# A Mamba-2 scan followed by a gated MLP: seven-product matmuls in three more steps, state updates moved to GpSimd, and another order of loads and of the head

## The chip, the cores and the metric

The kernel runs on one NeuronCore of a Trainium2 chip. Its engines work side by side, each through its own instructions in order: TensorE (PE in the profile, its weight loads PEld), VectorE (DVE), ScalarE (ACT), GpSimd (POOL) and SyncE (SP), which issues DMA transfers; ACT's queue can issue them too. The metric is device time in microseconds (us) of one execution, the median of several runs. Less is better.

## What is computed

The reference has two parts. The first is a chunked state-space scan over 4 batches, 8 heads and 768 positions, with a state of 16 x 32 per head:

```python
L = np.exp(cum[:, :, :, None] - cum[:, :, None, :]) * causal
M = np.einsum('bhin,bhjn->bhij', Cc, Bc) * L
y_intra = np.einsum('bhij,bhjd->bhid', M, xc)
y_inter = np.einsum('bhin,bhnd->bhid', Cc, state) * decay_to_i[:, :, :, None]
y[:, :, sl] = y_intra + y_inter
state = decay_full[:, :, None, None] * state + np.sum(Bx, axis=2)
```

Its output, as 3072 tokens of 256 features, goes through the second part, with w_in of 256 x 2048 and w_out of 2048 x 256, all in fp32:

```python
h = x @ w_in
g = h * np.cos(h)
return (g @ w_out).astype(np.float32)
```

## The kernel before

The sequence is cut into six chunks of 128 positions (NC = 6), each of two halves of 64 (W = 64). For each chunk the MLP runs 16 steps (NF = 16), numbered n = 16 c + f with chunk c and step f in it. A step multiplies 256 columns of w_in with half of the chunk's tokens (512 columns of the result, hp, in PSUM), forms the gate, and multiplies it with w_out into o. While chunk c goes through the MLP, the scan of chunk c + 1 is worked in between.

The order of every engine is written out by hand, in the loop over n from line 1114. In a step PE does hp of step n (`first`, L672, or `first7`, L772) and then o of step n - 2 (`second`, L808, or `seven`, L848; LAG = 2). Between them lies a chain over three engines: `wind_k` (ACT, L679), `wind_w` (DVE, L685), `gate` (ACT's sine, L694), `gated` (DVE, L699, writes gT), and from chunk 1 on `differ` (POOL, L724 to L727), which forms the four combinations gd of gT.

A product of two 2 x 2 block matrices takes eight block products, or seven with sums and differences of the blocks beforehand and of the results afterwards. From chunk 1 on `seven` does so for o: the differences of w_out are made once (`differ_w`), those of the gate by `differ`, and the results are summed per unit of eight steps (`rest`, L873, on POOL one part per step; then stores, L876). For hp `first7` does the same in the steps that `runs` (L1034) lists: steps 9 to 13 of chunks 2 to 4, and steps 1 to 13 of chunk 5. It needs the differences of w_in (`differ_in`, L743) and of y (`differ_y`, L754), and it ends in four additions on DVE (L785, L788, L790, L793) and a copy on ACT (L779). In a run the gate of step n is formed while hp of step n + 1 is made (`late`), and both pairs of PSUM banks with the tag "scan" belong to the run.

The scan's parts for chunk c + 1 are placed by the table `steps` (L1006), by step f of chunk c: `reach` (cumulated decays, DVE, L586), `turn` (transposes of B and C, DVE, L594), then one step later `turn2` (copies of C on ACT, L603, and the product rT on DVE, L605), `inner` (PE, L615), `weigh` (DVE, L477), `state` (the states carried on, DVE, L510), `decays` (scans of 512 columns, DVE, L387, from rows that `load_arow` fetches), `along` (loads of a for `reach`). `open2` (PE, L629, reads the states and rT) stands in step 14, `finish2` (PE, L641) in step 15.

SP's queue is in order too: a store that waits for its sum (L876) holds up the loads issued after it. `block_loads` places the loads of B and C for the transposes, `load` those of x and B by half, `rest_of_loads` those of the weights' last pieces, the rows of a and the third and fourth half.

The head, lines 285 to 302 and 909 to 946, is the scan of chunk 0 in two units of 64 positions. Loads: C by ACT in four parts (`load_c`), a, B, x and weights by SP (`fetch`). C is copied (L358 on POOL, a quarter on ACT, L918), turned (L407) and scaled (`take_c`, L411). `spread_a` (PE, L376) and `decays0` (DVE, L387) make the decays, `inner` (L468) the products of B and C, `weights` (L477) multiplies them. `finish0` (L489 to L537) makes y and the state, and its copy to yT is what hp reads. Weights arrive as words and are prepared by `grade` (ACT, L258 and L256; POOL, L259) and `join` (DVE, L271, L275; POOL, L283).

## Time and profile before

| what | us |
|---|---|
| median of 3 runs | 364.64 |
| lowest and highest run | 363.92, 365.25 |
| the profiled execution, its own time | 364.44 |
| its span, first to last instruction | 362.7 |

In the profile PE is busy in nearly every slice of the span but the first microseconds; the granted clock is 0.998 of full speed. Where the busy time of the costliest groups lies:

| line, engine | what | count | busy us | mean ns |
|---|---|---|---|---|
| L672 PE | hp, ordinary, 128x256 | 544 | 129.6 | 382 |
| L848 PE | o by seven products, 128x128 (largest group) | 474 | 66.0 | 275 |
| L772 PE | hp by seven products, 128x128 (largest group) | 168 | 23.4 | 276 |
| L685, L699 DVE | w and gT, 128x512 | 96 each | 65.8, 65.6 | 686, 683 |
| L724, L726, L727 POOL | gd | 79 each | 58.1, 39.6, 39.0 | 735, 501, 493 |
| L586 DVE | reach scans, 128x64 | 32 | 10.3 | 368 |
| L510 DVE | states, 128x64 (largest group) | 24 | 8.7 | 419 |
| L605 DVE | rT, 128x256 | 8 | 4.1 | 507 |

Matmuls overlap, so the mean of one is longer than the distance between two starts; a matmul in fp32 appears as two instructions. A line of the timeline or of the chain gives start and duration in us from the span's start.

### The profile page before, as it was taken

To read this page: it belongs to the slowest core of one execution; us is meant where nothing else is said; L and a number is where in the kernel's file an instruction comes from. 1 tells how busy PE (TensorE), PEld (TensorE's weight loads), DVE (VectorE), ACT (ScalarE), POOL (GpSimd) and SP (SyncE) were. 2 spreads that over 40 slices of the span, in tenths; PEclk is the share of its full clock that TensorE was granted. 3 is DMA by queue.
4 is the path that set the end of the run, shared out by engine and by line. 5 is a ranking of instruction groups with operands and counts; after the bars stand their busy time and mean duration, and the time that the engine had idled before them with its cause. 6 is when DMAs were issued, how large, how long until landed. Compare 5 with 4: busy or idle time off the path is not lost.

```text
span 362.7 us, 10240 instructions
## 1 busy us (share of the span) xinstructions
PE 357.0 (98%) x4070; PEld 326.0 (90%) x4070; DVE 276.0 (76%) x504; ACT 184.0 (51%) x352; POOL 239.7 (66%) x387
## 2 busy tenths in 40 slices
PE   8999999999999999999999999999999999999995
PEld 4788888889999999999989999999999999999995
DVE  7779998488876987878766877875776776688864
ACT  3597656544454346534536533545553544444552
POOL 5567767699666677674786666686666465475572
PEclk9999999999999999999999999999999999999999
DMA  7984997666583429113228202110001001001001
GB/s 138 246 284 141 189 196 122 85 125 98 134 129 58 99 51 135 14 34 76 53 53 119 23 3 75 28 33 11 0 2 31 0 3 33 0 3 29 3 17 44
DMA packets 96624, 26.43 MB, mean 73 GB/s; under 512 B 86624, under 2 KB 92480, under 8 KB 96576
## 3 DMA queue, kind: packets, MB, share of 16 engines
q1 hardware_dynamic: 95328, 25.38, 34.9%
q8 instruction: 32, 0.52, 0.6%
q10 hardware_dynamic: 1248, 0.39, 0.5%
q14 instruction: 16, 0.13, 0.1%
HBM read 22.36 MB, written 3.34 MB: 71 GB/s over the span
## 4 chain that ended last, share of the span: by engine, by line
PE 96%; DMA 2%; DVE 1%; issue 0%; ACT 0%; POOL 0%; DVEq 0%
PE o L848 35%; PE hp L672 33%; PE o L808 8%; PE m L772 7%; PE hp L772 5%; DMA bc<-in_C_dram 2%; PE y L641 2%; PE g L615 1%; PE y L489 1%; PE y L629 1%; PE g L468 1%; PE y L537 1%; PE y L527 1%; PE o L900 0%; PE tp L451 0%
## 5 line engine op out<-in xcount | busy, mean ns | idle before, releaser
L672 PE MATMUL hp<-yT,w_in 128*128 128x256 f32 x544 | 129.6, 382 | 0.1
L672 PEld LDWEIGHTS hp<-yT,w_in 128*128 128x128 f32 x544 | 99.0, 190 | 13.8 <-issue 1.4
L724 POOL TENSOR_TENSOR gd<-gT 128x256 f32<-128x256 f32 x79 | 58.1, 735 | 76.9 <-DVE gT L699 61.8
L694 ACT ACTIVATE w<-w,quarter 128x512 f32<-128x512 f32 x96 | 69.4, 723 | 65.8 <-DVE w L685 65.7
L685 DVE SCALAR_TENSOR_TENSOR w<-hp,k 128x512 f32<-128x512 f32 x96 | 65.8, 686 | 45.4 <-ACT k L679 45.2
L679 ACT ACTIVATE k<-hp 128x512 int32<-128x512 f32 x96 | 57.2, 596 | 68.6 <-PE hp L672 60.3
L699 DVE TENSOR_TENSOR gT<-hp,w 128x512 f32<-128x512 f32 x96 | 65.6, 683 | 12.2 <-ACT w L694 8.3
L848 PE MATMUL o<-words,gd 128*128 128x128 f32 x474 | 66.0, 275 | 0.0
L848 PEld LDWEIGHTS o<-words,gd 128*128 128x128 f32 x474 | 59.4, 192 | 0.0
L848 PE MATMUL o<-w_out,gT 128*128 128x128 f32 x316 | 50.4, 278 | 0.0
L848 PEld LDWEIGHTS o<-w_out,gT 128*128 128x128 f32 x316 | 45.4, 191 | 3.1
L726 POOL TENSOR_TENSOR gd<-gT,gd 128x128 f32<-128x128 f32 x79 | 39.6, 501 | 6.2
L727 POOL TENSOR_TENSOR gd<-gT,gd 128x128 f32<-128x128 f32 x79 | 39.0, 493 | 6.2
L848 PE MATMUL o<-w_out,gd 128*128 128x128 f32 x158 | 30.6, 276 | 0.0
L848 PE MATMUL o<-words,gT 128*128 128x128 f32 x158 | 30.6, 275 | 0.0
L808 PE MATMUL o<-w_out,gT 128*128 128x256 f32 x128 | 30.0, 380 | 0.0
L387 DVE TENSOR_TENSOR_SCAN lam<-arow,unit 128x512 f32<-128x512 f32 x20 | 29.9, 1496 | 0.1
L808 PEld LDWEIGHTS o<-w_out,gT 128*128 128x128 f32 x128 | 24.2, 190 | 3.6 <-POOL w_out L283 0.4
L848 PEld LDWEIGHTS o<-words,gT 128*128 128x128 f32 x158 | 24.0, 192 | 0.0
L848 PEld LDWEIGHTS o<-w_out,gd 128*128 128x128 f32 x158 | 24.0, 192 | 0.0
L772 PE MATMUL m<-m,words 128*128 128x128 f32 x168 | 23.4, 276 | 0.0
L772 PE MATMUL hp<-yT,w_in 128*128 128x128 f32 x112 | 21.7, 275 | 0.0
(130 smaller groups left out, 463.6 us busy)
## 6 DMA issues: line engine op xcount, KB each, us to landing
words<-in_moe_w_in_dram SPq DMA_DIRECT2D x8, 512.0 KB
words<-in_moe_w_out_dram SPq DMA_DIRECT2D x8, 512.0 KB
xr<-in_x_dram SPq DMA_DIRECT2D x24, 128.0 KB
arow<-a_cut SPq DMA_DIRECT2D x10, 256.0 KB
arow<-a_cut SPq DMA_DIRECT2D x10, 252.0 KB
out_dram<-sum SPq DMA_DIRECT2D x18, 128.0 KB
bc<-in_B_dram SPq DMA_DIRECT2D x24, 64.0 KB
blocks<-in_B_dram SPq DMA_DIRECT2D x16, 32.0 KB
```

The lines of the kernel that those rows point to most:

```text
L387: V.tensor_tensor_scan(out=lams[k][:, p, hs].rearrange(flat), data0=rows_.rearrange(flat), data1=unit0[:, hs].rearrange(flat), initial=0.0 ...
L672: PE.matmul(to_[:, e], lhsT=w_in[:, k, fs], rhs=y[:, k], start=(k == 0), stop=(k == KT - 1), skip_group_check=True)
L679: ACT.activation(k, hp[n], AF.Copy, bias=0.25, scale=INV_2PI)
L685: V.scalar_tensor_tensor(out=w, in0=hp[n], scalar=INV_2PI, in1=k, op0=ALU.mult, op1=ALU.subtract)
L694: ACT.activation(cos, cos, AF.Sin, bias=quarter, scale=TWO_PI)
L699: V.tensor_tensor(out=gT[n], in0=hp.pop(n), in1=cos, op=ALU.mult)
L724: G.tensor_tensor(out=d[:, 0:2], in0=g[:, 1:2].to_broadcast([P, 2, P]), in1=g[:, 3::-3], op=ALU.subtract)
L726: G.tensor_tensor(out=d[:, 2], in0=g[:, 0], in1=d[:, 0], op=ALU.subtract)
L727: G.tensor_tensor(out=d[:, 3], in0=g[:, 2], in1=d[:, 2], op=ALU.subtract)
L772: PE.matmul(dst[q], lhsT=w[q], rhs=y_[q], start=(q in (6, 1, 7)), stop=True, skip_group_check=True)
L808: PE.matmul(o[c, u][:, t], lhsT=g[:, 2 * e + t], rhs=w_out[:, 2 * j + e], start=(j == e == t == 0), stop=(j == NJ - 1 and e == 1), skip_gr ...
L848: PE.matmul(at[q], lhsT=a_[q], rhs=w[q], start=(j == 0 and q in starts), stop=(j == NJ - 1), skip_group_check=True)
```

## The change

Seven products for hp also in steps 2 to 4 of chunks 2 to 4 (`runs`). For that, the scan's parts in the table `steps` move: `reach` to steps 5 and 6, the transposes (`turn`) to the step before the chunk and step 1, the copies of C (`cut`) to steps 3 and 4, rT (`scale`) to steps 6 and 7 on POOL, the states to steps 2 and 8 on POOL (`add_state2`: a product in the step, the addition one step later), and the first `decays` from step 2 to 5. The differences of y for these steps are made on DVE in step 0, the others on POOL in steps 4, 5, 5 and 7; the output sums pause in steps 2 and 3. A reach is one scan over 260 columns, for which the rows of a in DRAM carry a leading zero (65 numbers per half) and `lead` has a tile of its own.

In the head C's fourth load goes to SP's queue, x is loaded before the first weights and half of it by ACT; C is copied whole on POOL, earlier, and turned before B; the first unit's y is opened by the state's sums; hp's first half stands before half of the second unit's `inner`; the first `join` writes in two halves. On SP's queue the rows and B of the fifth and sixth half change places, and chunk 0's outputs are stored by ACT.

```diff
...
-    ones = const.tile([P, P], FP32, name="ones")
-    V.memset(ones, 1.0)
+    lead = const.tile([P, NB, W + 1], FP32, name="lead")
...
-    a_all = dram.tile([NB, H, S], FP32, name="a_all")
+    a_all = dram.tile([NB, H, 2 * NC, W + 1], FP32, name="a_all")
...
-                    out=alongs[k][:, 2 * p + s, 1:],
-                    in_=a_all[2 * s + p, :, k * W:(k + 1) * W].unsqueeze(1).to_broadcast([H, N, W]))
+                    out=alongs[k][:, 2 * p + s],
+                    in_=a_all[2 * s + p, :, k].unsqueeze(1).to_broadcast([H, N, W + 1]))
...
-            along[c] = rows.tile([P, NB, P], FP32, tag="along", bufs=2, name="along")
+            along[c] = rows.tile([P, NB, 2 * (W + 1)], FP32, tag="along", bufs=2, name="along")
...
-                    out=along[c][rs, b], in_=a_all[b, hs, c * P:(c + 1) * P].unsqueeze(1)
-                    .to_broadcast([hs.stop - hs.start, N, P]))
+                    out=along[c][rs, b], in_=a_all[b, hs, 2 * c:2 * c + 2]
+                    .rearrange("h k i -> h (k i)").unsqueeze(1)
+                    .to_broadcast([hs.stop - hs.start, N, 2 * (W + 1)]))
...
-    lead, along1, reach1 = (ms[2][:, i * NB * (W + 1):(i + 1) * NB * (W + 1)]
-                            .rearrange("p (b i) -> p b i", b=NB) for i in range(3))
+    along1, reach1 = (ms[2][:, i * NB * (W + 1):(i + 1) * NB * (W + 1)]
+                      .rearrange("p (b i) -> p b i", b=NB) for i in range(1, 3))
...
-    def join(which, i, between=None):
+    def join(which, i, between=None, halves=False):
...
+            if halves:
+                for f in (slice(0, P), slice(P, 2 * P)):
+                    G.tensor_tensor(out=dst[:, :, f].bitcast(U32), in0=bits[:, :, f],
+                                    in1=last[:, :, f], op=ALU.add)
+                return
...
-    for b in range(NB):
-        load_c(b, nc.scalar)
+    for i in range(NB):
+        load_c(i, nc.scalar if i < NB - 1 else nc.sync)
...
+    load_x(0, 0)
+    load_x(0, 1, nc.scalar)
...
-    for s in range(2):
-        load_x(0, s)
...
+    c0 = loads.tile([P, 2, 2, 4, 2, N], FP32, tag="blocks", name="c0").rearrange(
+        "p a b c d n -> p (a b c d n)").rearrange("p (r h n) -> p r h n", r=4, h=H)
+    G.tensor_copy(out=c0.rearrange("p r h n -> p h r n"), in_=c4)
...
-    c0 = loads.tile([P, 2, 2, 4, 2, N], FP32, tag="blocks", name="c0").rearrange(
-        "p a b c d n -> p (a b c d n)").rearrange("p (r h n) -> p r h n", r=4, h=H)
-    G.tensor_copy(out=c0[:, 0:3].rearrange("p r h n -> p h r n"), in_=c4[:, :, 0:3])
...
-    def weigh_c(k, of):
+    def copy_c(of):
...
-        of(k, c)
+        of(1, c)
+        return c
+    def weigh_c(k, c):
...
-                i = k % 2 * W + W - 1
...
-                                       scalar=reach[k // 2, s][:, p, i:i + 1],
+                                       scalar=reach[k // 2][:, 2 * s + p, k % 2, W:],
...
-    def finish0(k):
+    def add_state2(k):
+        dec = scan.tile([P, 2, 2, 2 * D], FP32, tag="whole", bufs=1, name="whole")
+        flat = "p s q d -> p (s q) d"
+        G.tensor_tensor(out=dec.rearrange(flat), in0=after[k - 1].rearrange(flat),
+                        in1=reach[k // 2][:, :, k % 2, W:].to_broadcast([P, NB, 2 * D]),
+                        op=ALU.mult)
+        return lambda: G.tensor_tensor(out=after[k], in0=after[k], in1=dec, op=ALU.add)
+    def finish0(k, between=None):
...
+        at = [y[0][:, s, 3 * P:] for s in range(2)]
+        strip = lambda q, s: slice(32 * q, 32 * q + 32)
+        if k == 0:
+            sums(k, at, strip, start=True)
+        if between:
+            between()
...
-        sums(k, [y[0][:, s, 3 * P:] for s in range(2)], lambda q, s: slice(32 * q, 32 * q + 32),
-             start=(k == 0))
+        if k:
+            sums(k, at, strip)
...
-        else:
+        def take_y():
...
-        return take, add
-    def reaches(c, b):
-        s, p = divmod(b, 2)
-        if p == 0:
-            reach[c, s] = scan.tile([P, 2, P], FP32, tag="reach", name="reach")
-        for k in range(2):
-            i = slice(k * W, (k + 1) * W)
-            V.tensor_tensor_scan(out=reach[c, s][:, p, i], data0=along[c][:, b, i],
-                                 data1=ones[:, 0:W], initial=1.0, op0=ALU.mult, op1=ALU.mult)
-    turned, ys = {}, {}
+        return (take, add) if k else (take_y, take, add)
+    def reaches(c, s):
+        if s == 0:
+            reach[c] = scan.tile([P, NB, 2, W + 1], FP32, tag="reach", bufs=1, name="reach")
+        V.tensor_tensor_scan(
+            out=reach[c][:, 2 * s:2 * s + 2].rearrange("p b k i -> p (b k i)"),
+            data0=along[c][:, 2 * s:2 * s + 2].rearrange("p b i -> p (b i)"),
+            data1=lead.rearrange("p b i -> p (b i)"), initial=0.0, op0=ALU.mult, op1=ALU.add)
+    turned, ys, r2 = {}, {}, {}
...
-        tp = turned.pop((c, s))
+        tp = turned[c, s]
...
-        rT = scan.tile([P, 2, P], FP32, tag="rT", name="rT")
-        V.tensor_tensor(out=rT, in0=tp[:, 1], in1=reach[c, s], op=ALU.mult)
-        part[c, s] = (tp[:, 0], cT, rT)
+        part[c, s] = (tp[:, 0], cT)
+    def scale2(c, s, eng):
+        r2[c, s] = rT = scan.tile([P, 2, P], FP32, tag="rT", name="rT")
+        eng.tensor_tensor(out=rT.rearrange("p q (k i) -> p q k i", k=2),
+                          in0=turned.pop((c, s))[:, 1].rearrange("p q (k i) -> p q k i", k=2),
+                          in1=reach[c][:, 2 * s:2 * s + 2, :, 1:], op=ALU.mult)
...
-            bT, cT, _ = part[c, s]
+            bT, cT = part[c, s]
...
-                      rhs=part[c, s][2][r, p, k * W:(k + 1) * W], start=(k == p == 0), stop=False,
+                      rhs=r2[c, s][r, p, k * W:(k + 1) * W], start=(k == p == 0), stop=False,
...
-            nc.sync.dma_start(out=unit_rows[p, u], in_=ob[p * W:(p + 1) * W])
+            nc.scalar.dma_start(out=unit_rows[p, u], in_=ob[p * W:(p + 1) * W])
...
+    take_c, of_c = turn_c()
+    take_c(0)
...
-    ACT.copy(out=c0[:, 3:4].rearrange("p r h n -> p h r n"), in_=c4[:, :, 3:4])
...
-    take_c, of_c = turn_c()
...
-    take_c(0)
...
-    spread_a(1, 1, tag="h")
...
-    join("in", 0)
+    c1 = copy_c(of_c)
+    join("in", 0, halves=True)
...
+    yT0, take_s0, _ = finish0(0, lambda: spread_a(1, 1, tag="h"))
...
-    take_s0, _ = finish0(0)
+    weigh0(1)
...
+    weigh_c(1, c1)
+    yT0()
...
-    for t in range(2):
-        inner(1, t)
-    weigh0(1)
-    weigh_c(1, of_c)
-    la = const.tile([RB, NU, P], FP32, name="la")
+    inner(1, 0)
+    la = const.tile([RB, NU, 2, W + 1], FP32, name="la")
...
-        store_a(a_cut, cut)
+        nc.sync.dma_start(
+            out=a_cut.rearrange("(u b) h (c p) -> (b h c) u p", u=NU, p=P), in_=cut)
...
-        G.tensor_scalar(out=la, in0=a_in, **clip)
-    def store_a(dst, src):
-        nc.sync.dma_start(
-            out=dst.rearrange("(u b) h (c p) -> (b h c) u p", u=NU, p=P), in_=src)
+        G.memset(la[:, :, :, 0:1], 0.0)
+        G.tensor_scalar(out=la[:, :, :, 1:], in0=a_in.rearrange("p u (k i) -> p u k i", k=2), **clip)
...
-        store_a(a_all, la)
+        nc.sync.dma_start(
+            out=a_all.rearrange("(u b) h (c k) i -> (b h c) u (k i)", u=NU, k=2),
+            in_=la.rearrange("p u k i -> p u (k i)"))
...
-        for k in (4, 5):
-            for s in range(2):
-                load_b(k, s)
-    steps = {c: dict(reach=(5, 6), turn=(6, 7), inner=8, weigh=(9, 10), state=(-NF, 12),
-                     decays=(8, 11, 13, 14), along=(12, 13)) if c == 2 else
-             dict(reach=(1, 2), turn=(3, 4), inner=5, weigh=(6, 7), state=(0, 5),
-                  decays=(2, 8, 14, 15), along=(6, 7)) for c in range(2, NC)}
+        load_arow(4)
+    steps = {c: dict(reach=(5, 6), turn=(6, 7), cut=(7, 8), scale=(7, 8), inner=8, weigh=(9, 10),
+                     state=(-NF, 12), decays=(8, 11, 13, 14), along=(12, 13)) if c == 2 else
+             dict(reach=(5, 6), turn=(-1, 1), cut=(3, 4), scale=(6, 7), inner=5, weigh=(6, 7),
+                  state=(2, 8), decays=(5, 8, 14, 15), along=(6, 7)) for c in range(2, NC)}
...
-    runs = [*(range(NF * c + 9, NF * c + 14) for c in range(2, NC - 1)),
+    runs = [*(range(NF * c + f, NF * c + l) for c in range(2, NC - 1) for f, l in ((2, 5), (9, 14))),
...
-    late, at_ = [], {}
+    late, at_, adds = [], {}, []
...
-        to_ = at_["hp"] if i % 3 == (n > NF * (NC - 1)) else bank([P, TB], "hp", "h")
+        run = sevens.get(n, sevens.get(n - 1))
+        to_ = at_["hp"] if i % 3 == (len(run) != 5) else bank([P, TB], "hp", "h")
...
-        for q in range(2):
-            weights(1, q)
+        weights(1, 0)
...
-        first(0, lambda: states_of.extend(finish0(1)))
+        def unit1():
+            inner(1, 1)
+            weights(1, 1)
+            states_of.extend(finish0(1))
+        first(0, unit1)
...
-    for k in (2, 3):
-        G.memset(alongs[k][:, :, 0:1], 0.0)
...
-            if n in (NF - 4, NF - 3):
-                load_arow(n - NF + 8)
+            if n == NF - 6:
+                load_arow(5)
+            if n in (NF - 5, NF - 1):
+                for s in range(2):
+                    load_b(4 + (n == NF - 1), s)
...
+            for i in range(4 if f == 0 and 2 <= c < NC - 1 else 0):
+                differ_y(c, i, V, slice(0, 1))
...
-            for e, s in chunks_at(n - 1, "turn"):
+            for e, s in chunks_at(n, "cut"):
...
+            for e, s in chunks_at(n, "scale"):
+                if e == 2:
+                    scale2(e, s, V)
...
-            behind += [lambda k=2 * c - 1 + i: add_state(k) for c, i in chunks_at(n, "state")]
-            behind += [lambda c=c, b=2 * s + p: reaches(c, b) for c, s in chunks_at(n, "reach")
-                       for p in range(2)]
+            behind += [lambda k=2 * c - 1 + i: add_state(k) for c, i in chunks_at(n, "state")
+                       if c == 2]
+            behind += [lambda c=c, s=s: reaches(c, s) for c, s in chunks_at(n, "reach")]
...
-            for i, at in enumerate((4, 5, 6, 6) if 2 <= c < NC - 1 else ()):
+            for i, at in enumerate((4, 5, 5, 7) if 2 <= c < NC - 1 else ()):
...
-            if unsummed and (c > 1 or summed[0]):
+            for e, s in chunks_at(n, "scale"):
+                if e > 2:
+                    scale2(e, s, G)
+            for add in adds:
+                add()
+            adds[:] = [add_state2(2 * e - 1 + i) for e, i in chunks_at(n, "state") if e > 2]
+            if unsummed and (c > 1 and f not in (2, 3) or summed[0]):
...
```

## The prediction, made before the changed kernel ran

> **What bounds the kernel now.** I read the engines' busy shares first, then the chain that ended last, then single stages.
>
> ```profile
> PE 357.0 (98%) x4070; PEld 326.0 (90%) x4070; DVE 276.0 (76%) x504; ACT 184.0 (51%) x352; POOL 239.7 (66%) x387
> ...
> PE 96%; DMA 2%; DVE 1%; issue 0%; ACT 0%; POOL 0%; DVEq 0%
> ```
>
> The chain is TensorE (PE) for 96% of the span. So the time is the sum of what PE executes, plus the start before it has work. An edit elsewhere counts only if it makes PE wait or lets it start earlier. The chain of waits in chunk 2 shows the price of a step (start, us, what):
>
> ```profile
> 160.85 1.56 PE o L848 x14
> 162.41 1.73 PE hp L672 x8
> 164.14 1.56 PE o L848 x14
> 165.70 0.22 PE hp L772 x2
> 165.92 0.89 PE m L772 x8
> 166.82 0.45 PE hp L772 x4
> 167.26 1.56 PE o L848 x14
> ...
> 170.39 1.71 PE o L848 x14
> ...
> 179.92 1.56 PE o L848 x14
> ```
>
> A step is one hp and one o. With hp in the ordinary way (L672) it costs 1.73 + 1.56 = 3.29; with seven products (L772) 0.22 + 0.89 + 0.45 + 1.56 = 3.12, that is 0.17 less. The run of five from 164.14 to 179.92 takes 15.78 where five ordinary steps take 16.45: 0.67 less, not 5 x 0.17 = 0.85. So a run pays about 0.15 to 0.18 once, in its second step (the o of 1.71).
>
> The head, from the timeline (start, us, engine, line):
>
> ```profile
> 6.93 0.51 POOL L358 COPY c<-bc 128x384 f32<-128x384 f32 x1 [1.40 <-DMA bc<-in_C_dram]
> 8.62 0.69 DVE L387 TENSOR_TENSOR_SCAN lam<-a_ps,unit 128x256 f32<-128x256 f32 x1 [0.69 <-PE a_ps L376]
> 8.91 0.67 ACT L258 ACTIVATE mag<-words 128x512 f32<-128x512 f32 x1
> 9.67 0.61 POOL L259 TENSOR_SCALAR mag<-mag 128x512 f32<-128x512 f32 x1 [1.02 <-ACT mag L258]
> 9.81 1.29 DVE L477 TENSOR_TENSOR m<-g,lam 128x512 f32<-128x512 f32 x2 [0.50 <-PE g L468]
> 11.02 0.42 DVE L271 TENSOR_SCALAR mag<-mag 128x512 uint32<-128x512 uint32 x1
> ```
>
> C lands late, GpSimd (POOL) copies it at 6.93, the turned C reaches the weights (L477) at 9.81, and from there VectorE (DVE) works without a pause through L271, L275, the scans and the second unit's weights. PE becomes dense at 17.67, that is 6.65 after L271.
>
> **Part 1, seven products in steps 2 to 4 of chunks 2 to 4.** Nine steps, each 0.17 less: 1.53. Three more runs, each with one entry at 0.15: 0.45 back. Net **-1.1**. Bounds: -1.5 if a run entered at step 2 pays nothing (there the output copies have the ACT queue without a k conversion ahead of them), and -0.6 if each pays twice, at entry and at exit.
>
> **Part 2, what pays for it on DVE.** A seven-product step adds four DVE instructions: 0.29 (L785) + 0.42 (L788) + 0.43 (L790) + 0.29 (L793) = 1.43, so 4.3 for three steps, and four differences of half size, bounded by the 0.29 of L785 and the 0.68 of the full-size L754: 1.2 to 2.7. It removes eight state updates (8 x 0.42 = 3.4), two rT products (1.0) and replaces eight reach scans (8 x 0.37 = 2.9) by two of 260 columns (2 x 1.15, L442). Balance: 5.5 to 7.0 added, 5.0 removed, on some 56 us per chunk of which DVE is busy 44. Steps 2 to 4 become exactly like steps 9 to 13, since reaches, transposes, states and rT leave them: 0.69 + 0.68 + 1.43 = 2.8 in 3.12. I take **0**. The cover is slack. In the runs of today gd is ready 0.4 to 0.6 before the third product of o reads it (gd's first subtraction ends at 173.36, the o that needs it starts at 173.50 and reads it four PE instructions later); outside them the distance is 2 to 4 us. Should DVE lag more than that, PE waits for the excess.
>
> **Part 3, what moves to POOL.** Per chunk: two state decays and two additions (4 x 0.73, the row of L566) and two rT (2 x 0.73): 4.4. They fall with the output sums, now in steps 4 to 7, and the differences of y. Count from the first hp of step 2 (0). hp of step 5 starts at 9.5, gT(4) ends at 13.4, gT(5) behind a 1.44 scan at 16.0. POOL: gd(4) 13.6 to 15.4; gd(5) 16.1 to 17.9; two differences and a sum (1.64) to 19.5; gd(6) 19.9 to 21.7; rT and sum to 23.1; gd(7) to 24.9; difference, rT and sum (1.64) to 26.6; state product to 27.3. gT(8) ends at 27.8 and o of step 8 reads gd at 29.05. So POOL is free 0.5 before gT(8) arrives, and gd's first subtraction, 0.73 from 27.95, ends at 28.7, 0.35 ahead of PE. I take **0**, but this is the thinnest cover in the change, and the trace shows what can eat it:
>
> ```profile
> 185.74 1.44 DVE L387 TENSOR_TENSOR_SCAN lam<-arow,unit 128x512 f32<-128x512 f32 x1
> ...
> 186.17 1.25 POOL L726 TENSOR_TENSOR gd<-gT,gd 128x128 f32<-128x128 f32 x1
> 187.50 0.46 POOL L727 TENSOR_TENSOR gd<-gT,gd 128x128 f32<-128x128 f32 x1
> ```
>
> Beside a scan that reads two SBUF operands the POOL subtraction took 1.25, its twin afterwards 0.46. Steps 5 to 8 hold two reach scans and two decay scans: each can cost POOL 0.8. The first 0.9 goes into the idle 0.5 and the 0.35; two such meetings (1.6) would cost PE 0.7 per chunk, 2.1 in all.
> The Trainium skill ("SBUF — State Buffer", section "Who interferes with whom") speaks against this part more sharply: a DVE instruction with two SBUF inputs and a GpSimd instruction that reads SBUF exclude each other, and the loser stands still until the other is over. By it four scans of 1.15 to 1.44 could hold POOL for about 5 us per chunk, an estimate that would turn the change into a loss of some 10 us; the row agrees that there is a block (0.8 lost beside a 1.44 scan), but it shows most scans passing beside idle POOL.
>
> **Part 4, the head.** C's fourth load leaves the ACT queue, where it was issued at 2.99 and held back the copy to 6.93, and goes second on SyncE's (SP) queue, at about 1.2. The chain has C arriving 3.9 after the issue of the last load. With the third ACT issue at 1.7 as the last, and no more than that latency, C is there at 5.6 or earlier. B's loads stand one issue (0.4) later on SP, but B is now turned after C. ACT issues half of x in place of C's fourth load and has its table load (1.28) still before its first work at about 6.5. The copy is now whole on POOL (0.51 x 4/3 = 0.68) and put before two along1 products (1.23) and the own copy. Then it is no longer C that counts: DVE has four scans of weights to make before L477 and a fifth in order. Third scan 6.36 to 7.05, fourth by about 8.0 (its spread now behind six transposes), fifth to 8.7, L477 at 8.7 to 10.0: 1.1 earlier. But the next DVE instruction, L271, needs the first weight words. They are now queued behind x (2 x 128 KB, one half on ACT's queue) and C's last load. The DMA view shows 147 GB/s while x moved: 0.9 us for each half. The words' rate (292 GB/s in the stretch 6 to 7) falls at about 7.2; later by one or two halves gives 8.1 to 9.0, and some 0.5 until an engine is released (a: last data at 2.2 in that view, DVE at 2.68). ACT 0.67, POOL 0.61 and hand-overs of 0.15 bring L271 to 10.0 to 10.9; I take 10.4, 0.6 before today's 11.02. Behind it nothing shrinks by much: L275, two scans, reach, rT, the y matmuls are the same, and hp's first half now stands before half of the second unit's g, which only fills PE's waits. So PE is dense at about 17.05: **-0.6**. Bounds: -1.1 (words there in time) and +0.3 (x, C and words together saturate the queues, L271 at 11.3).
>
> **Part 5, the rest.** Removed: the memset of ones (0.17) and two small memsets, under the head's DMA waits: 0. Two output stores of chunk 0 issued from ACT, 4 issues of about 0.65 in steps 16 and 17, where gd is 1.9 to 2.9 ahead of PE: 0. Loads reordered on SP: arow(4) earlier, bc(4) and bc(5) later, a_all rows of 65 numbers instead of 64. DMA is busy 0.73 from 18 to 50 us and no compute engine waits for a transfer after the head: 0; without that cover the price is a DVE wait on arow or blocks. The blocks of the second half are now turned at step 1 instead of 4. SP issues the last of them at 189.5 in chunk 2, landing some 3 us later, and DVE would want them at about 198: 5 us of cover.
>
> **Sum.** -1.1 + 0 + 0 - 0.6 = -1.7. The profiled execution took 364.44 (span 362.7): 362.7 after. The median of the runs is 364.64, 0.2 above it, so **362.9**. A measurement of this kernel can tell about 0.3% (1.1 us) from no change.
>
> **Rivals.** *A, POOL takes over in steps 5 to 9* (slower): gd late, PE waits at o of steps 6 to 9. For: the 1.25 row and POOL's thin cover. Against: the same mixture in steps 13 to 15 today (two gd sets and two scans) makes no PE wait. Three meetings per chunk slip 2.4, less 0.85 of cover = 1.55, times 3 = 4.7: 364.6 - 1.7 + 4.7 = 367.6. It decides against the change from 1.7 + 1.1 = 2.8 us on, some 0.9 of wait per chunk. *B, the head gives nothing and the entries cost double* (no change): words land late, L271 at 11.2 or after. For: x now precedes the words. 364.6 - 0.6 + 0.2 = 364.2. *C, both bounds good:* -1.5 - 1.1 = 362.0. For: the free entry at step 2 and the slack before L271.
> That steps 2 to 4 do not become seven-product steps is excluded by the table of runs, which gets those three steps.
>
> **Chances.** Forecast 0.46 (its own range 362.3 to 363.5), C 0.16, B 0.18, A 0.20. Faster 0.46 + 0.16 = 0.62, no change 0.18, slower 0.20. Range: from 361.5, half a us below C, to 365.4, which takes in B and A's case of two meetings (362.9 + 2.1 = 365.0); A's worse half, some 0.12, and a head better than C stay outside.
>
> **What would show it.** Right: 37 steps with seven products instead of 28; steps 2 to 4 of chunks 2 to 4 at 3.12; PE dense from about 17.1; L271's first start near 10.4. Wrong: PE gaps before o in steps 6 to 9 with POOL busy without a break (A); ACT's first conversion of words released by a DMA after 9.5 (B); a PE gap in steps 0 or 1 behind a turned block or a y difference (part 5 or 2).

## The result and the profile after

The changed kernel is slower. Its median is 374.37 us (371.77 to 376.26, six executions) beside 364.64 us of the kernel before (363.92 to 365.25). The ratio on record, which is not formed from the two medians, is 1.0257, 95% interval 1.0213 to 1.0302. The profiled execution is the slowest of the six: it took 376.26 us, and its mean granted clock, 0.989, is the lowest of the six. Its span is 374.5 us where it was 362.7 us: 11.8 us to explain, 2 us more than lie between the medians. (One of the eight executions of e3 below ran at 0.749 of the clock and took 456.28 us; e3's median and ratio leave it out, with it the median is 366.04.)

The page of the changed kernel, with the rows of busy time, the granted clock in 40 slices and the chain that ended last:

```profile
PE 359.4 (96%) x4124; PEld 328.3 (88%) x4124; DVE 278.6 (74%) x497; ACT 184.5 (49%) x360; POOL 254.0 (68%) x405
...
PEclk9789999999999999999999999999999999999999
...
PE 70%; DVE 7%; POOL 7%; SPq 5%; DMA 4%; issue 3%; ACT 3%; ACTq 0%; POOLq 0%; DVEq 0%
```

PE held 96% of the chain before and holds 70% now: other engines and SP's queue stand in it, so PE waits. Its busy time rose by 2.4 us although the new products are cheaper; the clock row shows a reason: each digit stands for 9.4 us, and the second and third are 7 and 8, where the row of the kernel before has full clock.

Where the time went is read from the start of hp of every step n in both traces. The difference between the two starts is flat where nothing is lost, and jumps where PE waits:

| place | jump, us |
|---|---|
| head, first dense hp | +3.08 |
| the o that follows hp(18) and the o that follows hp(19) | +1.64 and +2.05 |
| entry of chunk 2's new run (before hp(34), hp(35)) | +0.77 and +0.24 |
| hp of step 9 in chunks 2, 3 and 4 | +1.61, +1.61, +0.18 |
| eight steps of the new runs | -0.16 each |
| before hp(64) and before hp(80) | +0.43 and +1.01 |
| all other jumps together and the end | +0.5 |

The first four rows are 11.2 us, and each has its place in the timeline. In the lines below the changed kernel has its own line numbers: hp is L699 and L799 (seven products), o is L875, k L706, the store of chunk 0's output L843, the differences of y L781, gd L751 to L754, the scans L392, the product with g L485.

The head of the changed kernel in the timeline (start, us, engine, line; in brackets the idle time before and what ended it):

```profile
8.06 1.26 DVE L485 TENSOR_TENSOR m<-g,lam 128x512 f32<-128x512 f32 x2
...
9.62 0.67 ACT L258 ACTIVATE mag<-words 128x512 f32<-128x512 f32 x1 [2.69 <-DMA words<-in_moe_w_in_dram]
...
11.02 0.43 DVE L271 TENSOR_SCALAR mag<-mag 128x512 uint32<-128x512 uint32 x1 [1.70 <-POOL mag L259]
...
12.83 0.71 PE L432 MATMUL a_ps<-m 128*128 128x260 f32 x2 [1.33 <-DVE lam L392]
...
14.06 1.71 PE L699 MATMUL hp<-yT,w_in 128*128 128x256 f32 x4
...
17.64 1.12 PE L549 MATMUL y<-rT,state 32*64 32x64 f32 x28 [0.81 <-DVE m L485]
...
20.24 1.21 PE L699 MATMUL hp<-yT,w_in 128*128 128x256 f32 x2
```

C came early as intended: the product with g starts at 8.06 (9.81 before). But the words landed later, ACT read them at 9.62 (8.91 before), and L271 starts at 11.02, to the hundredth where it was. VectorE stood idle 1.70 us in between. Then PE waits twice, and four matmuls of hp take 1.71 us where they took 1.13: the granted clock falls to half at 14.47.

ScalarE's queue in steps 16 to 18 of the changed kernel (ACTq is the issue of a transfer):

```profile
80.11 0.57 ACT L841 COPY ob<-o 128x512 f32<-128x512 f32 x1
83.30 1.47 ACTq L843 DMA_DIRECT2D out_dram<-ob  x2
84.82 0.60 ACT L706 ACTIVATE k<-hp 128x512 int32<-128x512 f32 x1 [4.13 <-DMA blocks<-in_C_dram]
...
87.40 2.39 ACTq L843 DMA_DIRECT2D out_dram<-ob  x2
89.84 0.60 ACT L706 ACTIVATE k<-hp 128x512 int32<-128x512 f32 x1 [2.47 <-DMA out_dram<-ob]
```

The copy ended at 80.68 and the store was issued at 83.30. In between nothing runs on ACT, and k, which stands behind the store, starts 4.13 us after the engine's last work. The releaser is a load of C for the transposes, which has nothing to do with the output.

Step 9 of chunk 2:

```profile
172.91 1.21 DVE L392 TENSOR_TENSOR_SCAN lam<-arow,unit 128x512 f32<-128x512 f32 x1
...
173.01 1.37 POOL L753 TENSOR_TENSOR gd<-gT,gd 128x128 f32<-128x128 f32 x1
...
174.45 0.46 POOL L754 TENSOR_TENSOR gd<-gT,gd 128x128 f32<-128x128 f32 x1
174.86 0.45 POOL L781 TENSOR_TENSOR m<-yT,m 128x128 f32<-128x128 f32 x1
...
175.37 0.49 PE L799 MATMUL m<-m,w_in 128*128 128x128 f32 x2 [1.34 <-POOL m L781]
```

The fourth difference of y, placed in step 7, stands behind gd(7) on POOL; gd's subtraction took 1.37 beside a scan (0.46 alone), and the first product of step 9 that needs the difference waits 1.34 us.

The entry of chunk 2's new run:

```profile
142.98 2.15 DVE L781 TENSOR_TENSOR m<-yT 128x128 f32<-128x128 f32 x2
...
143.39 1.60 POOL L770 TENSOR_TENSOR words<-w_in,words 128x640 f32<-128x640 f32 x1
...
145.06 1.34 DVE L781 TENSOR_TENSOR m<-yT,m 128x128 f32<-128x128 f32 x2
...
148.70 0.46 PE L799 MATMUL hp<-yT,w_in 128*128 128x128 f32 x2 [0.60 <-DVE gT L726]
```

Four differences of 128x128 on VectorE hold its queue from 142.98 to 146.40, the first two of them beside a POOL instruction on 128x640; w and gT follow late.

### The profile page after: what moved, and what is told of

Same layout as the page of the kernel before. It is cut to its first block, busy times and chain, and to the rows that moved or that the text cites. A ratio compares the mean times of both kernels' runs of the same rounds, so it can differ in the third digit from the quotient of the medians.

```text
span 374.5 us, 10363 instructions
## 1 busy us (share of the span) xinstructions
PE 359.4 (96%) x4124; PEld 328.3 (88%) x4124; DVE 278.6 (74%) x497; ACT 184.5 (49%) x360; POOL 254.0 (68%) x405
## 4 chain that ended last, share of the span: by engine, by line
PE 70%; DVE 7%; POOL 7%; SPq 5%; DMA 4%; issue 3%; ACT 3%; ACTq 0%; POOLq 0%; DVEq 0%
PE o L875 27%; PE hp L699 18%; PE m L799 8%; PE hp L799 7%; PE o L835 4%; POOL gd L751 2%; SPq L150 2%; DMA words<-in_moe_w_in_dram 1%; SPq L107 1%; DVE gT L726 1%; POOL gd L753 1%; DVE w L712 1%; PE y L668 1%; PE g L642 1%; ACT k L706 1%
## 5 line engine op out<-in xcount | busy, mean ns | idle before, releaser
L699 PE MATMUL hp<-yT,w_in 128*128 128x256 f32 x472 | 113.6, 385 | 2.0 <-DVE gT L726 1.9
L751 POOL TENSOR_TENSOR gd<-gT 128x256 f32<-128x256 f32 x79 | 60.1, 761 | 74.0 <-DVE gT L726 55.3
L699 PEld LDWEIGHTS hp<-yT,w_in 128*128 128x128 f32 x472 | 86.5, 191 | 14.6 <-issue 3.5
L706 ACT ACTIVATE k<-hp 128x512 int32<-128x512 f32 x96 | 57.1, 595 | 57.1 <-PE hp L699 41.2
L875 PE MATMUL o<-words,gd 128*128 128x128 f32 x474 | 66.7, 276 | 1.6 <-ACT ob L841 1.4
L875 PEld LDWEIGHTS o<-words,gd 128*128 128x128 f32 x474 | 59.6, 192 | 2.2 <-ACT ob L841 1.6
L875 PE MATMUL o<-w_out,gT 128*128 128x128 f32 x316 | 50.4, 278 | 0.0
L753 POOL TENSOR_TENSOR gd<-gT,gd 128x128 f32<-128x128 f32 x79 | 44.3, 561 | 6.2
L875 PEld LDWEIGHTS o<-w_out,gT 128*128 128x128 f32 x316 | 44.7, 191 | 2.6
L754 POOL TENSOR_TENSOR gd<-gT,gd 128x128 f32<-128x128 f32 x79 | 37.0, 468 | 6.2
L799 PE MATMUL m<-m,words 128*128 128x128 f32 x222 | 30.9, 275 | 0.0
L875 PE MATMUL o<-w_out,gd 128*128 128x128 f32 x158 | 30.8, 277 | 0.0
L875 PE MATMUL o<-words,gT 128*128 128x128 f32 x158 | 30.6, 275 | 0.0
L392 DVE TENSOR_TENSOR_SCAN lam<-arow,unit 128x512 f32<-128x512 f32 x20 | 30.5, 1527 | 0.0
L812 DVE TENSOR_TENSOR m<-m 128x128 f32<-128x128 f32 x37 | 10.8, 292 | 26.5 <-PE m L799 22.4
L799 PE MATMUL hp<-yT,w_in 128*128 128x128 f32 x148 | 28.7, 275 | 0.6 <-DVE gT L726 0.6
L799 PEld LDWEIGHTS m<-m,words 128*128 128x128 f32 x222 | 27.8, 192 | 0.0
```

The costliest lines, as they stand in the source:

```text
L392: V.tensor_tensor_scan(out=lams[k][:, p, hs].rearrange(flat), data0=rows_.rearrange(flat), data1=unit0[:, hs].rearrange(flat), initial=0.0 ...
L699: PE.matmul(to_[:, e], lhsT=w_in[:, k, fs], rhs=y[:, k], start=(k == 0), stop=(k == KT - 1), skip_group_check=True)
L706: ACT.activation(k, hp[n], AF.Copy, bias=0.25, scale=INV_2PI)
L751: G.tensor_tensor(out=d[:, 0:2], in0=g[:, 1:2].to_broadcast([P, 2, P]), in1=g[:, 3::-3], op=ALU.subtract)
L753: G.tensor_tensor(out=d[:, 2], in0=g[:, 0], in1=d[:, 0], op=ALU.subtract)
L754: G.tensor_tensor(out=d[:, 3], in0=g[:, 2], in1=d[:, 2], op=ALU.subtract)
```

## The experiments

Times are medians; the ratio is to runs of the kernel before on the same chip, whose median lay between 364.07 and 364.12 in all four sets (e1 to e4, e5 to e8, e9 to e12, e13 to e15). Where two kernels of different sets are compared it is by ratio.

| label | median us | ratio, 95% interval |
|---|---|---|
| e1 | 364.70 | 1.0020 (1.0011 to 1.0030) |
| e2 | 365.38 | 1.0031 (1.0019 to 1.0042) |
| e3 | 365.79 | 1.0059 (1.0035 to 1.0083) |
| e4 | 364.85 | 1.0022 (1.0009 to 1.0035) |
| e5 | 368.18 | 1.0115 (1.0099 to 1.0131) |
| e6 | 367.75 | 1.0108 (1.0090 to 1.0127) |
| e7 | 369.37 | 1.0149 (1.0133 to 1.0165) |
| e8 | 362.49 | 0.9963 (0.9950 to 0.9976) |
| e9 | 363.07 | 0.9973 (0.9962 to 0.9984) |
| e10 | 363.64 | 0.9986 (0.9975 to 0.9997) |
| e11 | 363.95 | 1.0004 (0.9987 to 1.0021) |
| e12 | 363.30 | 0.9973 (0.9963 to 0.9984) |
| e13 | 362.80 | 0.9967 (0.9955 to 0.9980) |
| e14 | 362.21 | 0.9952 (0.9938 to 0.9966) |
| e15 | 362.64 | 0.9962 (0.9950 to 0.9975) |

**e1: the stores alone, on the kernel before.**

```diff
-            nc.sync.dma_start(out=unit_rows[p, u], in_=ob[p * W:(p + 1) * W])
+            nc.scalar.dma_start(out=unit_rows[p, u], in_=ob[p * W:(p + 1) * W])
```

> The kernel before, with one edit: chunk 0's four output stores are issued by ACT instead of SP. Theory (a store's issue on ACT waits for an older transfer to land, and the k conversion behind it waits too): PE stands still before o of steps 16 and 17 for 1.6 to 2.1 us each as in the changed kernel, time 367 to 369. Rival (the stall of the changed kernel comes from its other reorderings of the queues): 364.6, no gap above 0.3 us.

364.70 us, 0.6 us more, and no jump at all from n = 18 to 20. The theory as it stood fell: the stores do not cost 3.7 us by themselves. Where the 0.6 us lie the trace does not show: its execution took 364.48 us, as long as the profiled one of the kernel before (364.44). ScalarE's queue in e1:

```profile
76.25 0.57 ACT L814 COPY ob<-o 128x512 f32<-128x512 f32 x1
76.85 1.37 ACTq L816 DMA_DIRECT2D out_dram<-ob  x2
78.27 0.60 ACT L679 ACTIVATE k<-hp 128x512 int32<-128x512 f32 x1 [1.45 <-PE hp L672]
```

The store goes out at once, and k is released by hp. The trace's records name the semaphore that a store raises when it lands, and show ScalarE waiting for that same semaphore ahead of the store. The transfer that had used it last stands on SP's queue. In e1 ScalarE was ready for the store at 76.82, and that transfer had been issued at 72.62, 4.2 us earlier. In the changed kernel ScalarE was ready at 80.68, the transfer was issued at 80.73, and the wait ended at 83.25, 2.5 us after its issue.

**e6: the stores with the changed order of SP's queue, on the kernel before.**

```diff
-            nc.sync.dma_start(out=unit_rows[p, u], in_=ob[p * W:(p + 1) * W])
+            nc.scalar.dma_start(out=unit_rows[p, u], in_=ob[p * W:(p + 1) * W])
...
-        for k in (4, 5):
-            for s in range(2):
-                load_b(k, s)
+        load_arow(4)
...
-            if n in (NF - 4, NF - 3):
-                load_arow(n - NF + 8)
+            if n == NF - 6:
+                load_arow(5)
+            if n in (NF - 5, NF - 1):
+                for s in range(2):
+                    load_b(4 + (n == NF - 1), s)
```

> The kernel before with two parts of the change together: the output stores issued from ScalarE's queue, and SyncE's queue in the changed order (arow(4) at the end of the loads after the head, arow(5) at n = 10, the B loads of units 4 and 5 at n = 11 and 15). The first part alone gave 364.70 us (+0.6). Theory (a store on ScalarE waits until the transfer that held its completion semaphore before has landed, and the reordered SyncE queue is what makes that transfer late): PE gaps of 1 to 2 us each come back in front of o of n = 16 to 20, and the time is 366 to 368.5 us. Rival (SyncE is late in the changed kernel for another reason, its head or its larger loads): no PE gap over 0.3 us there, 364.3 to 365.2 us.

367.75 us, jumps of 1.39 and 1.98 us before hp(19) and hp(20). ScalarE's queue in e6 repeats that of the changed kernel:

```profile
79.22 1.44 ACTq L816 DMA_DIRECT2D out_dram<-ob  x2
80.70 0.60 ACT L679 ACTIVATE k<-hp 128x512 int32<-128x512 f32 x1 [3.89 <-DMA blocks<-in_C_dram]
...
83.28 2.33 ACTq L816 DMA_DIRECT2D out_dram<-ob  x2
85.66 0.60 ACT L679 ACTIVATE k<-hp 128x512 int32<-128x512 f32 x1 [2.40 <-DMA xr<-in_x_dram]
```

Here ScalarE was ready at 76.81 and the transfer that held the semaphore had been issued at 76.55, only 0.26 us earlier; it is a load of C now, and was a load of B in e1. So the stores alone cost 0.6 us, and 3.7 us with the new order of SP's queue. That order alone was not run; e4 below has it with the stores on SP, and no jump at n = 18 to 20. It is not told apart how much comes from SP being later (that load of C was issued at 75.29 in e1) and how much from the semaphores falling to other transfers. An estimate from these rows: the wait in e6 ended at 79.17, 2.6 us after the load's issue, so had the store of e1 waited for the same load, it would have been held until about 77.9, for 1.1 us and not for the 2.4 of e6. Neither alone seems to be the whole.

**e5 and e3: the stores back on SP, then also the fourth difference a step earlier.** Both stand on the changed kernel; e3 has both edits, e5 the first alone.

```diff
-            nc.scalar.dma_start(out=unit_rows[p, u], in_=ob[p * W:(p + 1) * W])
+            nc.sync.dma_start(out=unit_rows[p, u], in_=ob[p * W:(p + 1) * W])
...
-            for i, at in enumerate((4, 5, 5, 7) if 2 <= c < NC - 1 else ()):
+            for i, at in enumerate((4, 5, 5, 6) if 2 <= c < NC - 1 else ()):
```

> The changed kernel with one edit undone: the output stores are issued from SyncE's queue again (the y differences stay at steps 4, 5, 5, 7, the new head and everything else stay). Theory (the two edits cost by themselves, each its own waits): the two PE gaps in front of o of steps 16 and 17 (1.64 and 2.05 us) go, the two of 1.61 us at step 9 of chunks 2 and 3 stay; the time is 374.4 - 3.7 = about 370.5 us. Rival (the fourth difference's wait is only there because the stores had delayed what stands before it, and goes with them): about 366 us, as with both edits undone (366.04).

> The changed kernel with two edits: chunk 0's stores on SP again, and the fourth difference of y in step 6 instead of 7. Theory: minus 3.7 for the stores and minus 1.6 twice for the waits of step 9 in chunks 2 and 3, that is 366 to 369 by the head's clock (before: 364.6). Rival (POOL is short of time as such in steps 5 to 9, so the wait moves to gd): o of steps 6 to 9 waits instead and at most 4 us are won, 370 or more.

e5 took 368.18 us: the jumps at n = 18 to 20 are gone, those at step 9 are there as before (1.60, 1.60 and 0.17 us), so they are no consequence of the stores. It is 2.3 us under what the theory said, because its head ran at full clock and cost 0.6 us in place of 3.1 in the trace. Against the two executions of the changed kernel with a mean clock of 1.000 (371.77 and 372.19 us) it is 3.6 and 4.0 us less, as the theory has it for the stores. e3 took 365.79 us: the earlier difference is worth 2 us more by the ratios, where 3.2 were expected; e4's trace shows new waits at step 11, where a part of the rest can lie.

**e2 and e4: the new head alone on the kernel before, and the old head in e3.** The edit is the head's part of the change, put in for e2 and taken out for e4; its core:

```diff
-    for b in range(NB):
-        load_c(b, nc.scalar)
+    for i in range(NB):
+        load_c(i, nc.scalar if i < NB - 1 else nc.sync)
...
+    load_x(0, 0)
+    load_x(0, 1, nc.scalar)
     fetch("in", 0)
-    for s in range(2):
-        load_x(0, s)
...
-    for t in range(2):
-        inner(1, t)
+    inner(1, 0)
```

> The kernel before, with the head of the changed kernel alone (loads, C's copy, the order of the units). Theory (PE is idle long enough in the new head for the clock to be halved in some executions): profile shows a stretch of about 6.8 us at half clock between 10 and 22 us or not, by execution; with it PE is dense at about 20.2 instead of 17.7 and the time is 367 to 368, without it 364 to 365; the runs spread over more than 2 us. Rival (the prediction's sum): 364.0, dense at 17.1, no spread.

> As the run before, and with the head of the kernel before. Theory: no half clock, PE dense at 17.7; what remains is the seven products' gain of 0.49 per chunk (1.5) less the wait at the entry of chunk 2 (1.2): 364.0 to 364.8, the time of before. Rival (seven products in steps 2 to 4 lose more elsewhere, for example in finish2 of chunk 5, 1.1 in the profile): 366.

e2 is 1.3 us over the kernel before by the medians (0.4 to 0.5 in its trace, which is of one of the faster executions): the new head loses. The half clock that the theory expected in some executions came in none of the seven (mean clock 0.998 to 1.000), so this loss is the head's own. e4 is 0.9 us under e3 by the medians and 0.2% over the kernel before. What is left in e4's trace: +0.66 and +0.23 at the entry of chunk 2's run, +0.40 and +0.55 at step 11 of chunks 2 and 3, against runs of seven that give back 0.49 each in chunks 3 and 4. GpSimd and PE in chunk 3 of e4 (gd is L736 to L739, rT L616, o L860):

```profile
213.19 1.25 POOL L738 TENSOR_TENSOR gd<-gT,gd 128x128 f32<-128x128 f32 x1
...
214.93 1.12 POOL L736 TENSOR_TENSOR gd<-gT 128x256 f32<-128x256 f32 x1
...
218.60 1.12 POOL L736 TENSOR_TENSOR gd<-gT 128x256 f32<-128x256 f32 x1
...
221.16 0.68 POOL L616 TENSOR_TENSOR rT<-turned,reach 128x256 f32<-128x256 f32 x1
...
223.30 1.25 POOL L738 TENSOR_TENSOR gd<-gT,gd 128x128 f32<-128x128 f32 x1
...
228.59 0.94 PE L860 MATMUL o<-words,gd 128*128 128x128 f32 x6 [0.28 <-POOL gd L738]
```

Four of gd's instructions take 1.12 to 1.25 (0.73 and 0.46 alone): each ran beside a scan on VectorE (these start at 212.75, 214.69, 218.37 and 222.79). POOL has no pause from 212.4 to 229.7, and o waits for gd.

**e7: filler matmuls in the head of e5**, six of 128x128 on ones into a part of a PSUM tile that nothing reads.

```diff
     take_b = turn_b(1, tp_b)
+    for i in range(6):
+        fill(y_of[0][:, i % 2, 2 * P:3 * P].unsqueeze(1))
```

> e5 (the changed kernel with its stores on SyncE's queue) with six filler matmuls of 128x128 on ones, written to a part of a PSUM tile that nothing reads, placed behind the turning of B of unit 1, where PE waits 1.33 us for VectorE's scans in the head. Theory (the half clock from 14.5 to 21.3 us follows a stretch of 3.4 us in which PE was busy 2.1 us): the granted clock stays full through the head, PE is dense with hp at 18 to 19 us in place of 20.2, and the time is 1 to 2.6 us under e5's. Rival (the half clock has another cause, such as power, or comes in some executions whatever PE does): the clock falls as before, and the time is e5's to within 0.4 us. If e5's own profile shows no half clock, the two times decide: a difference under 0.4 us then says that the filler does nothing.

369.37 us, 1.2 us over e5. e5 itself had run at full clock, so the filler had nothing to save and only lengthened the head (PE dense 1.3 us later). It decides nothing on the clock.

**e8: two parts of the change fewer.** e4 without the run of chunk 2 (and what belongs to it in steps 0, 2 and 3 of that chunk), and with rT on VectorE.

```diff
-    runs = [*(range(NF * c + f, NF * c + l) for c in range(2, NC - 1) for f, l in ((2, 5), (9, 14))),
+    runs = [*(range(NF * c + f, NF * c + l) for c in range(2, NC - 1) for f, l in ((2, 5), (9, 14))
+              if (c, f) != (2, 2)),
...
-                if e == 2:
-                    scale2(e, s, V)
+                scale2(e, s, V)
...
-            for e, s in chunks_at(n, "scale"):
-                if e > 2:
-                    scale2(e, s, G)
```

> The changed kernel with the old head, the stores on SyncE's queue and the y differences at steps 4, 5, 5, 6 (364.85 us so far, 0.2% over before), and two further parts undone: chunk 2 has no seven products in steps 2 to 4 (and no y differences on VectorE in its step 0), and rT of chunks 3 and 4 is on VectorE again. Theory (what is left over before is the entry of chunk 2's first run, 0.66 + 0.23 us, and GpSimd's queue, full from step 5 on, that holds gd back by 0.40 and 0.55 us at steps 11 of chunks 2 and 3): all of it goes, the two remaining runs keep 0.49 us each, and the time is 363.2 to 363.9 us, under before by 0.2 to 0.3%. Rival (VectorE, with the two multiplications of rT back beside gT, becomes late in its place; or the waits at step 11 come from the state additions): 364.3 to 364.9 us.

362.49 us, under the kernel before by 0.37%, and under the 363.2 to 363.9 us of the theory. No jump at n = 34 and 35, none at step 11; in chunk 3 rT is all that differs from e4, so the 0.55 us were POOL's two products.

**e9: chunk 2's run again, but POOL's 128x640 out of its way**, on e8.

```diff
-            for start, js in zip((2 * NF - 5, 3 * NF - 3, 4 * NF - 3),
+            for start, js in zip((2 * NF - 6, 3 * NF - 3, 4 * NF - 3),
```

> e8 (old head, stores on SyncE's queue, y differences at steps 4, 5, 5, 6, rT on VectorE, no first run in chunk 2: 362.49 us) with chunk 2's run of steps 2 to 4 put back, and GpSimd's first block of w_in differences (four of 128x640) one step earlier. Theory (the run's entry cost 0.66 to 0.77 and 0.23 us because VectorE's four y differences ran beside the last 128x640 of GpSimd): with that instruction out of the way the entry is free, hp of n = 34 and 35 starts with no new shift, the run keeps its 3 x 0.16 us, and the time is 362.0 us. Rival (the four y differences delay w and gT of that step by their own length, whatever stands beside them; chunks 3 and 4 hide them because they have no such full GpSimd in the step): the entry's 0.7 to 0.9 us come back, 362.9 us.

In the trace the entry is free, as the theory has it: it costs +0.00, two of its steps give 0.16 each, and VectorE's four differences take 1.34 and 0.74 in place of 2.15 and 1.34. The time is not what was expected: 363.07 us, a ratio no better than e8's. In its trace 0.16 and 0.55 us are lost at the end of chunk 3. The 0.55 us are no wait for GpSimd: PE stops for 0.28 us between two matmuls of one o (246.20 to 246.47) with no releaser in the profile, marked "issue". e14 below has the same run without that loss.

**e10: e8 without any run in steps 2 to 4** (the entries `(2, 5)` taken out of `runs`, and no differences in step 0).

> e8 without any run of seven products in steps 2 to 4: chunks 3 and 4 lose theirs too, and nothing is differenced in step 0. What is left of the change is the moves alone (state additions on GpSimd, the merged scans, the B loads and arow in the new order on SyncE, the new places of the turns). Theory (a run gives 3 x 0.163 us and its entry costs nothing in chunks 3 and 4): e8 + 0.98 = 363.5 us, and the shift against before stays flat over steps 2 to 4 of chunks 3 and 4. Rival (the entry's work on VectorE costs something elsewhere in the chunk): under 363.3 us.

363.64 us, and a flat shift over steps 2 to 4 of chunks 3 and 4. Between the ratios 0.9986 and 0.9963 lie 0.8 us for two runs, near the 0.98 worked out.

**e11, e12, e13: what in the head loses.** e11 is e8 with the whole new head. e12 puts x behind the first words again. e13 also puts all of unit 1's `inner` and `weights` ahead of hp(0) again.

```diff
-    load_x(0, 0)
-    load_x(0, 1, nc.scalar)
     fetch("in", 0)
+    for s in range(2):
+        load_x(0, s)
...
-    inner(1, 0)
+    for t in range(2):
+        inner(1, t)
...
-            inner(1, 1)
-            weights(1, 1)
```

> e8 with the new head put back (all of it). Theory (the new head loses by itself, because the words of the first weight block land behind x and its VectorE pass still starts at about 11 us, 362.49 + 0.5 to 1.3 us): 363.0 to 363.8 us, first words read at 9.4 to 9.6 us and PE dense with hp at 18.0 us or later. Rival (the loss in the other versions came from something else than the head): 362.3 to 362.7 us.

> e11 (e8 with the new head) with one part of the new head undone: x of units 0 and 1 is issued behind the first weight block again, both on SyncE's queue, as before. Theory (the order of the loads puts the words 0.7 to 1.0 us later, and that takes back what the earlier C copy gave): the first words are read at 8.6 to 9.0 us, the first VectorE pass on them starts at or under 10.4 us, PE is dense with hp at 17.1 to 17.5 us, and the time is 0.5 to 1.0 us under e11's. Rival (the head loses by the order of its program, with decays, y and g of units 0 and 1 behind one another, not by the words): within 0.3 us of e11, or over it.

> e12 with the second half of inner(1) and of its weights put back to where they were, ahead of hp(0). Theory (the head was predicted rightly but for two things: the words came later, which e12 undid, and the halving of inner(1), which puts g of its second half behind four matmuls of hp(0) and leaves PE waiting 0.81 us for VectorE): PE is dense with hp at 17.0 to 17.2 us, no wait of over 0.3 us on the second product with g, and the time is 0.6 to 0.8 us under e12's, 0.2 to 0.6 us under e8's. Rival (something else in the new program holds the y matmuls of unit 1 back, the gap only moves): PE dense at 17.7 us or later, the time within 0.3 us of e12's.

e11: 363.95 us, 0.41% or 1.5 us over e8 by the ratios, with the words read at 9.78; two of its twelve executions had a lower clock (last section). e12: 363.30 us, 0.65 us under e11. Its head in the timeline:

```profile
8.07 0.69 ACT L258 ACTIVATE mag<-words 128x512 f32<-128x512 f32 x1
...
10.18 0.42 DVE L271 TENSOR_SCALAR mag<-mag 128x512 uint32<-128x512 uint32 x1
...
13.62 1.13 PE L699 MATMUL hp<-yT,w_in 128*128 128x256 f32 x4
...
15.41 0.69 DVE L485 TENSOR_TENSOR m<-g,lam 128x512 f32<-128x512 f32 x1 [0.96 <-PE g L476]
...
16.16 0.68 PE L549 MATMUL y<-rT,state 32*64 32x64 f32 x28 [0.81 <-DVE m L485]
...
17.87 0.92 PE L699 MATMUL hp<-yT,w_in 128*128 128x256 f32 x3
```

L271 starts at 10.18, as early as the prediction hoped, and PE is still dense only at 17.87 (17.1 to 17.5 was expected): the second half of g stands behind hp(0)'s first four matmuls, VectorE waits 0.96 for it and PE 0.81 for VectorE. In e13 that wait is gone, and the bound has moved once more:

```profile
9.06 0.43 DVE L271 TENSOR_SCALAR mag<-mag 128x512 uint32<-128x512 uint32 x1
9.71 0.43 PE L497 MATMUL y<-xr,sc 64*32 64x64 f32 x24 [0.74 <-DMA xr<-in_x_dram]
...
17.46 1.35 PE L699 MATMUL hp<-yT,w_in 128*128 128x256 f32 x5
```

Now x is late, because it stands behind the words. PE is dense at 17.46, between what the theory (17.2 at most) and the rival (17.7 at least) said. The 0.6 to 0.8 us under e12 that were expected did not come: the ratios differ by 0.2 us. e13 took 362.80 us where e8, run again beside it as e15, took 362.64: with both faults mended the new head gains nothing over the old one.

**e14 and e15: the two together, and e8 again.** e14 is e13 with e9's two edits (`if (c, f) != (2, 2)` removed, the w_in differences a step earlier).

> e13 with the run of steps 2 to 4 in chunk 2 and the w_in differences one step earlier, as in e9. Theory (the run gains 0.49 us and its entry is free, but e9 lost some of it again near the end of chunk 3, 0.16 + 0.55 us in its profile, which may be chance): 0 to 0.5 us under e13. Rival (that loss belongs to the later state of GpSimd with the run in): 0.2 to 0.7 us over e13.

> e8 once more, on the chip of e13 and e14. It was 362.49 us beside 364.08 us of the kernel before (a ratio of 0.9963 with 0.9950 to 0.9976): 0.995 to 0.998 is expected again.

e14: 362.21 us, 0.9952 (0.9938 to 0.9966), the fastest of all, 0.6 us under e13, where 0 to 0.5 were expected. Its run in chunk 2 gives three times 0.16 us at a free entry, and of e9's later losses 0.18 us is left. e15 repeats e8's ratio.

## Why the prediction was wrong

It forecast 362.9 us, faster, with a range of 361.5 to 365.4 us. It was 374.37, slower.

**Part 5 failed most: "Two output stores of chunk 0 issued from ACT, 4 issues of about 0.65 in steps 16 and 17, where gd is 1.9 to 2.9 ahead of PE: 0".** The issues were counted, and they are about that long (1.47 us for two). What was not asked is what a transfer waits for before it is issued. The store waits for the semaphore that it is going to raise, which an earlier transfer of SP's queue still held, and on ScalarE that wait holds k, w and gT of the next step: 3.69 us. The reordering of SP's queue was priced at 0 in the next sentence, beside compute engines that wait for loads; that a store on another queue waits for them too joins the two edits. e1 (the stores alone, +0.6), e6 (both, +3.7) and e4 (the new order alone of the two, no jump) show that only the pair has the price.
The Trainium skill ("DMA: Bandwidth & Descriptors", section "Anatomy of one DMA — SWDGE (gpsimd) path") says that a semaphore wait of a transfer happens on the sequencer that issues it, before dispatch. The section is about transfers that GpSimd issues, and this one is ScalarE's; the row agrees, with ScalarE's queue held from 80.68 to 83.25.

**Part 3 took 0 for POOL and was wrong by its reader.** The count followed gd up to o of step 8, and found 0.35 us of cover. It also listed the fourth difference of y, ending at about 25.4 in its own count, but did not ask who reads it: the fourth product of step 9, some 24.8 after hp of step 2 starts (24.36 from hp(34) to hp(41) in the trace of before, less 0.5 for the three new steps, plus 0.9 to the product). So the plain count was already 0.6 short there, and the scan beside gd(7) added 0.9. The jumps at step 9 are 3.4 us in all. Rival A named the place and the mechanism (POOL blocked beside scans in steps 5 to 9) and priced it at 4.7 us; it looked at gd, which was to blame only in e4, for 0.40 and 0.55 us. The prediction's row of 1.25 was the right guide to the size of one meeting: in chunk 3 of e4 four meetings cost gd 0.4 to 0.8 us each, 2.4 us in all. The 5 us per chunk that it estimated from the rule on SBUF ports, and the loss of 10 us in all, were too high; the 0 was too low.

**Part 4, the head: -0.6 forecast, about +0.5 to +1.3 measured at full clock (e2), +3.08 in the profiled execution.** Its upper bound, +0.3 with "L271 at 11.3", was the nearest to the truth. "I take 10.4" failed at the words, read at 9.62 and not at about 9.0 (10.4 less the 1.43 us that it put down for ACT, POOL and the hand-overs); and even the true 10.18 of e12 did not give 17.05, because "hp's first half now stands before half of the second unit's g, which only fills PE's waits" is wrong: VectorE waits for that g, and PE for VectorE.

**Part 1 was right in mechanism and in one bound.** A step in seven products saves 0.16 us, and the entry is free, the good bound of -1.5, except in chunk 2, where part 2's differences on VectorE met POOL's 128x640 (e9 and e14 show it by moving that instruction). Part 2's 0 fails there, for 1.01 us in the changed kernel.

Not settled: 1.01 us before hp(80) and 0.43 us before hp(64) are in the profile of the changed kernel and not in that of e5, which has the same code there but for the stores. At both places PE stops without a releaser ("issue"), as in e9: for 0.88 us in the middle of `finish2`'s small matmuls before hp(80), for 0.17 us between two matmuls of one o before hp(64). What makes it stop is not shown. The six executions of the changed kernel differ by 4.5 us, of which these and the clock can be the larger part.

## What to carry to other kernels

A store that is moved to a compute engine's queue takes its wait along: look in the trace for the transfer that used its semaphore last, on whichever queue, and ask what stands behind the store. For each operation that is moved later, write down its first reader and the time of that read, not only the next link of the busiest chain; and put no full engine's work beside scans that block it. Price edits in pairs where they share a queue: 0.6 us for the store alone became 3.7 us with the new order of loads.

## What the hardware showed that was not expected

**The clock halved after a window in which PE was more than half busy.** In the head of the changed kernel the clock was at half from 14.47 to 21.30, that is for 6.83 us. The row of the 3.41 us ahead of that, half as long and still at full clock, and the row of the same stretch of e5 (length; PE, PEld, DVE, ACT, POOL busy; clock, DMA share, GB/s):

```profile
11.06:14.47 3.41, 2.08 (x27) 1.31 (x23) 3.38 (x6) 3.20 (x9) 1.92 (x3) 1.00 0.87 165
```

```profile
11.06:14.47 3.41, 2.53 (x60) 1.67 (x53) 3.38 (x6) 3.09 (x9) 1.99 (x3) 1.00 0.97 220
```

With PE busy 2.08 us of 3.41 (1.80 in e11) the granted clock fell to half in the next stretch; with 2.53 (e5) and 3.03 (e2) it did not. No single gap of PE was over 1.33 us (1.61 in e11). PE's busy share alone does not decide it, though. In e6, behind the late stores, PE was busy less, and the clock stayed full there and in the next stretch:

```profile
86.16:89.57 3.41, 1.59 (x15) 1.43 (x14) 2.97 (x5) 2.19 (x6) 0.06 (x1) 1.00 0.72 115
```

What sets the head's stretch apart from this one is not shown. In e11 two of twelve executions had a mean clock of 0.989 to 0.991 and took 366.11 and 366.49 us, the others 363.3 to 364.4: some 2.3 us for one such fall.
The Trainium skill ("TensorE: Matmul & The Clock Gate", section "Part 1: The HAM clock gate (the "warmup" mystery)") has the clock fall after an idle window of about 3.4 us; here it fell after one that was 53 to 61% busy, and did not after one of 47% (e6); the measurement decides.

**Moving a load changed who was late.** In the head the words, x and C are loaded side by side; in the changed kernel the DMA share is 1.06 from 3 to 6.5 us and 1.13 from 6.5 to 10, so the DMA engines had no room to spare. x first put ACT's reading of the words at 9.62 (8.91 before) and left VectorE idle 1.70 us; the words first (e13) put them at 7.64 and left PE waiting 0.74 us for x. e12 and e13 were dense 0.20 us after and 0.21 us before the 17.67 of the kernel before.
